# A fused chunk-attention and ELU-FFN kernel: the attention of early tiles in quarters with one transfer of v each, and the loads of later tiles' q and k taken apart

## Chip, cores and metric

One core of a Trainium2 chip runs the whole kernel. The metric is the device time of one execution in microseconds, as the median of several runs; lower is better.

## What is computed

Attention within chunks of 64 tokens, 8 heads of width 64, followed by a feed-forward layer with ELU, all in float32. q and k are drawn 5.7 times larger than in the function below.

```python
B, H, S, D = 8, 8, 576, 64            # q, k, v; chunk = 64, so 9 chunks per sequence
scores = scale * np.matmul(q_c, k_c.transpose(0, 1, 2, 4, 3))
scores = scores - np.max(scores, axis=-1, keepdims=True)
attn = np.exp(scores)
attn = attn / (np.sum(attn, axis=-1, keepdims=True) + 1e-09)
out = np.matmul(attn, v_c)            # then [B, S, H*D] flattened to x: 4608 tokens x 512
h = x @ w_in                          # 512 x 2048
g = np.where(h > 0.0, h, np.exp(np.minimum(h, 0.0)) - 1.0)
return g @ w_out                      # 2048 x 512
```

The weights come as float64 words; the kernel turns each into a float32 value and splits it into two parts (names ending in `_hi` and `_lo`) whose products TensorE takes at its fast rate; x and the hidden values are split in the same way, and `three` (L431) issues three matmuls for one product.

## The kernel before

The 4608 tokens are 36 tiles of 128, that is two chunks each, in nine blocks of four tiles. Attention of a block's tiles is worked out while the block before it is in the feed-forward part, except for the first four tiles, which have nothing to hide behind: this is the **start**. The order of the work on PE, ACT, DVE and SP is written out by hand in strings, one item for one step of a generator, so each engine takes its instructions in just that order.

The start follows `LOADS` (order of the transfers on SP) and `START`. In `START` a digit is the next step of that tile's attention, `r` one step of weight preparation on ACT (`prepare_units`, L140 and L145), `d` one step of weight splitting, mostly on DVE (`split_units`, L160 to L188), and `wN` N transposes of a constant on PE, whose result is not used (`warm`, L677). `uN` in `LOADS` is weight unit N: a slice of `w_in` and, from unit 1, one of `w_out`. Unit u+2 is loaded from step `d` of unit u.

The attention of a tile (`early_attention`) has ten steps: 1 transposes of q and k on PE (L266); 2 copies out of PSUM on ACT (L275, L278), where k is spread over a zeroed tile of twice its size (`kbd`, `k_apart`) so that one matmul of 128 rows serves two heads; 3 scores (L313); 4 maximum and subtraction on DVE (L319, L333); 5 exp on ACT (L337), or with `by_head` eight exps that take the maximum and give the sum of a head each (L327); 6 sums, reciprocal and product on DVE (L339 to L341, L282); 7 four transposes of the result on PE (L286); 8 a copy on ACT (L289); 9 the product with v (L297); 10 x is put away by ACT (L423, L417), in the start with a second half on DVE (L424). The product with v reads v in an arrangement that takes four transfers (`load_v`, L230).

The first block follows `FIRST_BLOCK`: H is the hidden product of one of 16 slices of w_in, P the projection of the slice before, and a a step of the next block's tile, whose loads are issued at the second a of the tile before. In blocks 1 and 2, and from block 3 on, tiles 8 to 35 go through `later_attention`, which transposes q and k on DVE (L358), computes scores and x in quarters of 64 rows by 64 columns of PE (L364, L406), and turns the softmax through eight small transfers within the chip (L397) and a DVE transpose (L399).

From block 3 on the feed-forward part uses a scheme with seven products per pair of slices. Its operands are read from DRAM again for each block, in four transfers a pair (`load_operands`, L566, item `w`), which PE needs two pairs later. The strings for this are `PAIRS` (two pairs to a tile), `FIRST_PAIR`, `OPENING_PAIR` and `LAST_PAIR`. Item `L` issues the transfers of q and k of the next tile but one (`load_tokens`, L247: four for q and four for k, or eight and eight where the tile crosses the end of a sequence, as tiles 4, 13, 22 and 31 do); `l` issues v (L219); `n` is a step of the next tile, `a` one of the present tile. Outputs are stored from SP too (L481). SP works strictly in order.

Of the kernel before, what the change touches and what calls it, by code (L numbers as in the profile page):

```python
# [10 lines left out]
F32 = mybir.dt.float32  # L11
# [9 lines left out]
def kernel(  # L21
# [19 lines left out]
    nc = tc.nc  # L41
# [33 lines left out]
    ps_h = ctx.enter_context(tc.tile_pool(name="ps_h", bufs=2, space=bass.MemoryType.PSUM))  # L75
# [4 lines left out]
    k_apart = const.tile([P, NK, 2, P], F32, name="k_apart")  # L80
# [70 lines left out]
    def split_units():  # L151
# [13 lines left out]
        for u in range(NU):  # L165
# [13 lines left out]
            if u:  # L179
                yield from subtract(u - 1)  # L180
# [8 lines left out]
            yield  # L189
        yield from subtract(NU - 1)  # L190
# [10 lines left out]

    def chunk_of(n: int):
        b, s = divmod(n, S)
        return b, slice(s, s + C)
# [19 lines left out]
    def load_v(n0: int, pool):  # L224

        v_sb = pool.tile([P, NK, 2, D], F32, name="v_sb")
        for j in range(2):
            for c in range(2):
                b, ss = chunk_of(n0 + c * C)
                nc.sync.dma_start(  # L230
                    out=v_sb[j * C:(j + 1) * C, :, c, :],
                    in_=v[b, j::2, ss, :].rearrange("h s d -> s h d"),
                )
        return v_sb

    def load_tokens(n0: int, qk):
# [4 lines left out]
        for i, src in enumerate((q, k)):  # L241
# [18 lines left out]


    def front_tensor(q_sb, k_sb, kbd, at, psum):
        def transpose(src):
            ps = psum([P, NK, P])
            for hp in range(NK):
                nc.tensor.transpose(  # L266
                    out=ps[:, hp, :], in_=src[:, 2 * hp:2 * hp + 2, :], identity=ident
                )
            return ps

        q_ps = transpose(q_sb)
        k_ps = transpose(k_sb)
        yield
        qT = at.tile([P, NK, P], F32, name="qT")
        nc.scalar.copy(out=qT, in_=q_ps)  # L275
        for j in range(2):
            js = slice(j * D, (j + 1) * D)
            nc.scalar.copy(out=kbd[js, :, j, :], in_=k_ps[js])  # L278
        yield qT

    def back_tensor(a, z, v_sb, at, psum):
        nc.vector.tensor_tensor(out=a, in0=a, in1=z.broadcast_to([P, H, C]), op=ALU.mult)  # L282
        yield
        a_ps = psum([P, NK, P])
        for hp in range(NK):
            nc.tensor.transpose(out=a_ps[:, hp, :], in_=a[:, 2 * hp:2 * hp + 2, :], identity=ident)  # L286
        yield
        aT = at.tile([P, NK, P], F32, name="qT")
        nc.scalar.copy(out=aT, in_=a_ps)  # L289
        yield  # L290
        x_ps = psum([P, NK, P])
        for hp in range(NK):
            for c in range(2):
                cs = slice(c * C, (c + 1) * C)
                for j in range(2):
                    js = slice(j * D, (j + 1) * D)
                    nc.tensor.matmul(  # L297
                        x_ps[js, hp, cs], lhsT=v_sb[js, hp, c, :], rhs=aT[js, hp, cs],
                        start=True, stop=True,
                    )  # L300
        return x_ps

    def early_attention(tt: int, front, v_sb, kbd, at, psum, put, by_head: bool = False):

        next(front)
        yield
        qT = next(front)
        yield
        s_ps = psum([P, H, C])
        for hp in range(NK):  # L310
            for c in range(2):
                cs = slice(c * C, (c + 1) * C)
                nc.tensor.matmul(  # L313
                    s_ps[cs, 2 * hp:2 * hp + 2, :], lhsT=qT[:, hp, cs], rhs=kbd[:, hp, :, cs],
                    start=True, stop=True,
                )
        yield
        mx = sm.tile([P, H, 1], F32, name="mx")
        nc.vector.tensor_reduce(out=mx, in_=s_ps, axis=AX.X, op=ALU.max)  # L319
        a = at.tile([P, H, C], F32, name="a")  # L320
        z = sm.tile([P, H, 1], F32, name="z")
        if by_head:

            nc.vector.tensor_scalar_mul(mx, mx, -SCALE)
            yield
            for h in range(H):
                nc.scalar.activation(  # L327
                    out=a[:, h, :], in_=s_ps[:, h, :], func=AF.Exp, scale=SCALE,
                    bias=mx[:, h, :], accum_out=z[:, h, :],
                )  # L330
            yield
        else:
            nc.vector.tensor_tensor(  # L333
                out=a, in0=s_ps, in1=mx.broadcast_to([P, H, C]), op=ALU.subtract
            )
            yield
            nc.scalar.activation(out=a, in_=a, func=AF.Exp, scale=SCALE)  # L337
            yield
            nc.vector.tensor_reduce(out=z, in_=a, axis=AX.X, op=ALU.add)  # L339
        nc.vector.tensor_scalar_add(z, z, 1e-9)  # L340
        nc.vector.reciprocal(z, z)  # L341
        x_ps = yield from back_tensor(a, z, v_sb, at, psum)
        yield
        put((slice(None), slice(None), slice(tt * P, (tt + 1) * P)), x_ps)
        yield
# [673 lines left out]
```

## Time and profile before

| | us |
|---|---|
| Median of 3 runs (863.40, 864.01, 864.86) | 864.01 |
| The profiled execution's own time | 868.06 |
| Its span from the first to the last instruction | 866.30 |
| PE busy in that span | 847.7 (98%) |
| DVE, ACT, POOL busy | 508.9, 484.5, 217.4 |
| TensorE clock granted over the span | 0.994 of full speed |

All rows come from one profiled execution, whose time is 4.05 us above the median of the others. In rows of the timeline the first number is the start in us from the beginning of the span, the second the time from the start of the first to the end of the last instruction merged in the row, then come engine, line, operation, operands, the count, and in brackets the idle time before it with what ended it. PE is TensorE's matmuls, SPq the issue of transfers. Several rows of one engine overlap a little, so the distance from one start to the next is what an instruction costs.

### The profile page before, as it was taken

To read this page: it belongs to the slowest core of one execution; us is meant where nothing else is said; L and a number is where in the kernel's file an instruction comes from. 1 tells how busy PE (TensorE), PEld (TensorE's weight loads), DVE (VectorE), ACT (ScalarE), POOL (GpSimd) and SP (SyncE) were. 2 spreads that over 40 slices of the span, in tenths; PEclk is the share of its full clock that TensorE was granted. 3 is DMA by queue.
4 is the path that set the end of the run, shared out by engine and by line. 5 is a ranking of instruction groups with operands and counts; after the bars stand their busy time and mean duration, and the time that the engine had idled before them with its cause. 6 is when DMAs were issued, how large, how long until landed. Compare 5 with 4: busy or idle time off the path is not lost.

```text
span 866.3 us, 17307 instructions
## 1 busy us (share of the span) xinstructions
PE 847.7 (98%) x6622; PEld 732.8 (85%) x6622; DVE 508.9 (59%) x840; ACT 484.5 (56%) x933; POOL 217.4 (25%) x184
## 2 busy tenths in 40 slices
PE   7799999999999999999989999999999999999998
PEld 6678888888888888888878888888888988889997
DVE  5789996556766566456534674457556754542222
ACT  6799985344534346546635564556544645465443
POOL 2000003126223023224312242225222522252221
PEclk9899999999999999999999999999999999999999
DMA  7786552546467758887688868887869798557521
GB/s 192 198 256 198 186 151 74 163 127 198 151 220 227 222 171 252 255 241 222 196 254 265 249 214 260 258 253 222 279 202 271 214 289 271 191 195 240 171 86 49
DMA packets 156707, 180.47 MB, mean 208 GB/s; under 512 B 67024, under 2 KB 123344, under 8 KB 156624
## 3 DMA queue, kind: packets, MB, share of 16 engines
q1 hardware_dynamic: 156624, 179.36, 67.6%
q8 instruction: 52, 0.85, 0.4%
q14 instruction: 31, 0.25, 0.1%
HBM read 147.85 MB, written 24.12 MB: 199 GB/s over the span
## 4 chain that ended last, share of the span: by engine, by line
PE 90%; DMA 4%; SPq 2%; ACT 2%; DVE 1%; issue 0%; ACTq 0%
PE o L431 44%; PE h L431 41%; DMA st<-in_moe_w_out_dram 2%; PE ps_a L364 2%; DMA wi_hi<-a_dram 2%; PE ps_a L406 1%; SPq L219 1%; SPq L230 1%; PE ps_a L297 0%; PE ps_a L313 0%; SPq L119 0%; PE ps_a L266 0%; ACT st L140 0%; DMA y<-y 0%; ACT st L145 0%
## 5 line engine op out<-in xcount | busy, mean ns | idle before, releaser
L655 POOL TENSOR_TENSOR wi_lo<-e,wi_hi 128x512 fp32r<-128x512 f32 x84 | 108.6, 1293 | 331.5 <-ACT wi_hi L651 331.5
L431 PE MATMUL h<-xhi,wi_hi 128*128 128x256 f32 (+1 forms) x704 | 189.7, 315 | 0.0
L639 DVE TENSOR_TENSOR kept<-h,kept 128x256 f32<-128x256 f32 x144 | 60.9, 423 | 178.2 <-PE h L431 112.3
L634 ACT COPY kept<-h 128x256 f32<-128x256 f32 x192 | 70.2, 366 | 169.2 <-PE h L431 169.1
L431 PE MATMUL o<-wo_lo,wi_hi 128*128 128x512 f32 x384 | 152.5, 397 | 0.0
L431 PE MATMUL o<-wo_hi,wi_hi 128*128 128x512 f32 x384 | 152.3, 397 | 0.0
L431 PE MATMUL o<-wo_hi,wi_lo 128*128 128x512 f32 x384 | 149.7, 390 | 0.0
L431 PE MATMUL h<-xlo,wi_hi 128*128 128x256 f32 (+1 forms) x448 | 147.2, 329 | 0.0
L431 PEld LDWEIGHTS h<-xhi,wi_hi 128*128 128x128 f32 x704 | 124.0, 189 | 14.5 <-issue 0.3
L431 PE MATMUL h<-xhi,wi_lo 128*128 128x256 f32 (+1 forms) x448 | 131.4, 330 | 0.5 <-DVE wi_lo L160 0.5
L431 PEld LDWEIGHTS h<-xlo,wi_hi 128*128 128x128 f32 x448 | 84.5, 189 | 12.2 <-DVE xlo L424 0.2
L431 PEld LDWEIGHTS h<-wi_lo,wi_hi 128*128 128x128 f32 x576 | 81.8, 189 | 11.2 <-DMA wi_hi<-a_dram 2.2
L431 PEld LDWEIGHTS h<-xhi,wi_lo 128*128 128x128 f32 x448 | 79.7, 188 | 11.5 <-DVE wi_lo L160 0.9
L646 DVE SCALAR_TENSOR_TENSOR e<-e,kept 128x512 f32<-128x512 f32 x96 | 66.9, 697 | 36.2 <-ACT e L644 21.2
L431 PE MATMUL h<-wi_lo,wi_hi 128*128 128x256 f32 x576 | 85.0, 283 | 2.2 <-DMA wi_hi<-a_dram 2.0
L431 PEld LDWEIGHTS o<-wo_hi,wi_lo 128*128 128x128 f32 x384 | 72.3, 188 | 16.4 <-POOL wi_lo L655 0.3
L643 ACT ACTIVATE e<-kept 128x512 f32<-128x512 f32 x96 | 60.6, 632 | 34.7 <-DVE kept L639 34.6
L651 ACT CAST wi_hi<-e 128x512 fp32r<-128x512 f32 x96 | 59.8, 623 | 32.0 <-DVE e L646 31.6
L431 PE MATMUL o<-wo_hi,ghi 128*128 128x512 f32 x192 | 76.3, 397 | 0.0
L431 PEld LDWEIGHTS o<-wo_lo,wi_hi 128*128 128x128 f32 x384 | 73.8, 192 | 2.3
L507 POOL TENSOR_TENSOR kept<-wi_hi,wi_lo 128x512 f32<-128x512 f32 x16 | 20.8, 1323 | 216.7 <-DVE qT L358 132.6
L431 PEld LDWEIGHTS o<-wo_hi,wi_hi 128*128 128x128 f32 x384 | 72.7, 189 | 2.6
(100 smaller groups left out, 1379.7 us busy)
## 6 DMA issues: line engine op xcount, KB each, us to landing
wi_hi<-a_dram SPq DMA_DIRECT2D x128, 448.0 KB, 5.7
wi_lo<-a_dram SPq DMA_DIRECT2D x64, 448.0 KB, 5.5
kept<-in_q_dram SPq DMA_DIRECT2D x100, 128.0 KB, 7.2
kept<-in_k_dram SPq DMA_DIRECT2D x100, 128.0 KB, 4.9
st<-in_moe_w_in_dram SPq DMA_DIRECT2D x16, 512.0 KB, 4.2
st<-in_moe_w_out_dram SPq DMA_DIRECT2D x16, 512.0 KB, 4.9
a_dram<-kept SPq DMA_DIRECT2D x16, 512.0 KB, 4.3
y<-y SPq DMA_DIRECT2D x224, 32.0 KB, 1.9
```

What stands on the lines that cost most here:

```text
L219: nc.sync.dma_start(out=dst[p0:p0 + n], in_=src[b, :, s0:s0 + n, :].rearrange("h s d -> s h d"))
L230: nc.sync.dma_start(out=v_sb[j * C:(j + 1) * C, :, c, :], in_=v[b, j::2, ss, :].rearrange("h s d -> s h d"),)
L364: nc.tensor.matmul(scores[halves[c], j, hp, :], lhsT=qT[halves[j], hp, halves[c]], rhs=kT[halves[j], hp, halves[c]], start=True, stop=True,)
L406: nc.tensor.matmul(x_ps[halves[j], c, hp, :], lhsT=v_sb[halves[c], 2 * hp + j, :], rhs=turned[halves[c], j * NK + hp, :], start=True, stop ...
L431: nc.tensor.matmul(ps, lhsT=a, rhs=b, start=start, stop=stop, skip_group_check=onto)
L507: nc.gpsimd.tensor_tensor(out=out, in0=a, in1=b, op=op)
L634: nc.scalar.copy(out=out, in_=self.x)
L639: nc.vector.tensor_tensor(out=out, in0=self.y, in1=self.kept[kept], op=ALU.add)
L643: nc.scalar.activation(out=e, in_=c, func=AF.Relu, scale=-1.0)
L646: nc.vector.scalar_tensor_tensor(out=e, in0=e, scalar=-1.0, in1=c, op0=ALU.add, op1=ALU.max)
L651: nc.scalar.copy(out=ghi, in_=e)
L655: engine.tensor_tensor(out=glo, in0=e, in1=ghi.bitcast(F32), op=ALU.subtract)
```

## The change

The early tiles (0 to 7) take on the quarter scheme of the later ones. q and k are transposed into the two banks of one PSUM tile; k is copied as it is, without the spreading and the zeroed tiles; scores and the product with v are 64x64 quarters; the softmax is turned by sixteen 64x64 matmuls with a constant, in place of four transposes; v comes in one transfer with the form of q's. Two tiles of the start (2 and 3) use the exps by head. `LOADS` and `START` are rewritten, the start's PSUM is four tiles of two banks, the hidden products' PSUM is allocated after the start and no longer ahead of it, and the subtraction for weight unit 0 comes right after its copy. From block 3 on, `L` loads k of the next tile only and moves to the second pair of a tile, and a new item `M` at the end of that pair loads q of the tile after it.

```diff
-    LOADS = "q0 k0 q1 k1 k2 q2 u0 q3 k3 v3 v0 u1 v2 v1"
+    LOADS = "q0 k0 q1 k1 q2 k2 u0 v0 q3 k3 v1 v2 v3 u1"
+    BY_HEAD = (2, 3)
     START = (
-        "w13 0 0 1 1 0 1 0 2 1 0 2 2 0 r 3 0 1 d 2 3 3 2 1 2 0 0 3 2 0 r 1 w7 3 d 2 r 1 "
-        "2 3 r w1 d 3 3 d d 1 d 1 3 2 w8 3 r r d w1 d d d"
+        "w13 0 0 1 1 0 0 2 1 1 0 2 r r d 0 2 2 1 d 3 0 0 3 1 3 3 2 0 0 d 1 1 2 3 1 1 2 2 d 3 "
+        "2 2 r r d w4 3 3 3 d 3 r r d d d d"
     )
...
+    def multiply_v(x_ps, v_sb, aT):
+        for hp in range(NK):
+            for c, j in quarters:
+                nc.tensor.matmul(
+                    x_ps[halves[j], c, hp, :], lhsT=v_sb[halves[c], 2 * hp + j, :],
+                    rhs=aT[halves[c], j * NK + hp, :], start=True, stop=True,
+                )
...
+    def early_attention(tt: int, q_sb, k_sb, v_sb, kT, at, pool, put, by_head: bool):
+        both = pool.tile([P, 2, DM], F32, name="ps_a")
...
+        for i, to in enumerate((qT, kT)):
+            nc.scalar.copy(out=to, in_=both[:, i, :].rearrange("p (h t) -> p h t", h=NK))
+        yield
+        scores = first_halves(both)
+        score(scores, qT, kT)
+        yield
...
+        turned_ps = both[:, 0, :].rearrange("p (h t) -> p h t", h=H)
+        for h in range(H):
+            for half in halves:
+                nc.tensor.matmul(
+                    turned_ps[half, h, :], lhsT=a[half, h, :], rhs=ident[half, half],
+                    start=True, stop=True,
+                )
+        yield
...
-        "p1 c1 x1 Q p2 d1 w B Q p6 c2 B Q B x2 p5 w x3 n n Q p7 c3 d2 A w a Q Q L p4 c4 A w Q p3 d3 "
+        "p1 c1 x1 Q p2 d1 w B Q p6 c2 B Q B x2 p5 w x3 n n Q p7 c3 d2 A w a Q Q p4 c4 A w Q p3 d3 "
         "A A Q B",
-        "n a a p1 c1 Q p2 d1 w B Q p6 c2 B Q B n n p5 w Q n p7 c3 d2 A w n l Q Q p4 c4 A w Q p3 d3 "
-        "A A Q B w",
+        "n a a L p1 c1 Q p2 d1 w B Q p6 c2 B Q B n n p5 w Q n p7 c3 d2 A w n l Q Q p4 c4 A w Q p3 d3 "
+        "A A Q B w M",
...
                     elif item == "L":
                         if n + 1 < NB * NTT:
-                            loaded = load_tokens((n + 1) * P, place_of_tokens(n + 1))
+                            loaded = load_tokens((n + 1) * P, place_of_tokens(n + 1), (1,))
+                    elif item == "M":
+                        m = n + 2 - (g == 0)
+                        if m < NB * NTT:
+                            load_tokens(m * P, place_of_tokens(m), (0,))
```

`OPENING_PAIR` loses its `L` as the first string of `PAIRS` does, `LAST_PAIR` is changed like the second, and `FIRST_PAIR` has `M` in the place of `L`. `load_v`, the spread tiles and their memsets on POOL go.

## Rows read from the trace of the kernel before

**Rows 1.** Timeline of PE, end of the start and first block.
```profile
24.60 2.20 PE L297 MATMUL ps_a<-qT,v_sb 64*64 64x64 f32 x32 [3.19 <-DMA v_sb<-in_v_dram]
...
32.29 0.47 PE L431 MATMUL h<-xhi,wi_hi 128*128 128x512 f32 x1
...
35.73 0.66 PE L266 MATMUL ps_a<-ident,q_sb 128*128 128x128 f32 x4 [0.38 <-DMA q_sb<-in_q_dram]
...
40.80 1.09 PE L313 MATMUL ps_a<-k_apart,qT 128*64 128x128 f32 x16 [0.72 <-issue]
```
**Rows 2.** Timeline of SP in the start.
```profile
6.26 0.90 SPq L119 DMA_DIRECT2D st<-in_moe_w_in_dram  x1
...
18.00 6.92 SPq L230 DMA_DIRECT2D v_sb<-in_v_dram  x8
```
**Rows 3.** Busy time by stretch: PE, PEld, DVE, ACT, POOL, PE clock, DMA share, GB/s.
```profile
32.30:60.00 27.70, 25.77 (x153) 20.18 (x154) 24.25 (x34) 25.66 (x51) 0.00 (x0) 1.00 0.76 223
...
430.00:460.00 30.00, 26.31 (x208) 23.02 (x207) 11.02 (x21) 11.96 (x25) 6.38 (x5) 0.94 0.79 243
```
**Rows 4.** What PE waited for from 138 us to the end: total, times, longest.
```profile
PE h L431 <- DMA wi_hi<-a_dram: 2.0, 1, 2.0
PE ps_a L406 <- DVE turned L399: 0.9, 1, 0.9
PE h L431 <- DMA wi_lo<-a_dram: 0.8, 1, 0.8
```
**Rows 5.** Timeline of SP ahead of these waits.
```profile
417.93 8.70 SPq L247 DMA_DIRECT2D kept<-in_q_dram  x8
...
430.48 0.37 SPq L566 DMA_DIRECT2D wi_lo<-a_dram  x1
...
434.67 7.20 SPq L397 DMA_DIRECT2D y<-y  x8
```
**Rows 6.** Timeline of DVE: the values that the transfers at 434.67 move.
```profile
427.45 0.75 DVE L388 TENSOR_TENSOR y<-ps_a,z 128x256 f32<-128x256 f32 x2
```
**Rows 7.** Transfer issued at 6.26: count, KB, us from issue to landing.
```profile
st<-in_moe_w_in_dram SPq DMA_DIRECT2D x1, 512.0 KB, 5.9
```
**Rows 8.** Timeline of DVE: step 6 of one tile, then the next.
```profile
15.80 0.68 DVE L339 TENSOR_REDUCE z<-a 128x8 f32<-128x512 f32 x1
...
17.56 0.68 DVE L339 TENSOR_REDUCE z<-a 128x8 f32<-128x512 f32 x1
```
**Rows 9.** Timeline of ACT: a copy, a wide preparation, exps by head, what follows.
```profile
17.39 0.58 ACT L289 COPY qT<-ps_a 128x512 f32<-128x512 f32 x1
...
24.39 1.13 ACT L140 ACTIVATE st<-st 128x1024 f32<-128x1024 f32 x1 [2.52 <-DMA st<-in_moe_w_out_dram]
...
43.32 0.31 ACT L327 ACTIVATE a<-ps_a,mx 128x64 f32<-128x64 f32 x1 [0.17 <-DVE mx L324]
...
45.73 0.65 ACT L456 CAST ghi<-e 128x512 fp32r<-128x512 f32 x1
```
**Rows 10.** Timeline of PE: steps 3, 7 and 9 of an early tile with the matmul after each.
```profile
92.99 1.09 PE L313 MATMUL ps_a<-k_apart,qT 128*64 128x128 f32 x16
94.01 0.50 PE L431 MATMUL o<-wo_hi,ghi 128*128 128x512 f32 x1
...
99.59 0.60 PE L286 MATMUL ps_a<-ident,a 128*128 128x128 f32 x4
99.94 0.48 PE L431 MATMUL o<-wo_hi,ghi 128*128 128x512 f32 x1
...
105.61 1.15 PE L297 MATMUL ps_a<-qT,v_sb 64*64 64x64 f32 x32
106.69 0.50 PE L431 MATMUL o<-wo_hi,ghi 128*128 128x512 f32 x1
```
**Rows 11.** The same for scores in quarters of a later tile.
```profile
140.90 0.69 PE L364 MATMUL ps_a<-k_apart,qT 64*64 64x64 f32 x32
141.53 0.50 PE L431 MATMUL h<-xhi,wi_hi 128*128 128x512 f32 x1
```

More of the change, by code (lines that the diff above doesn't have):

```diff
@@ L189, in split_units @@
             yield
+            if u == 0:
+                yield from subtract(0)
         yield from subtract(NU - 1)
@@ L222, in load_heads, with load_tokens @@
         return dst
[L224 to L236, printed above, removed]
+    def load_tokens(n0: int, qk, which=(0, 1)):
         U = 4
-        for i, src in enumerate((q, k)):
+        for i in which:
+            src = (q, k)[i]
             for j in range(2):
@@ L281, in back_tensor @@
[L281 to L345, printed above, removed]
@@ L347, in later_attention @@
-    def later_attention(tt: int, qk, v_sb):
-        halves = [slice(i * C, (i + 1) * C) for i in range(2)]
-        quarters = [(0, 0), (1, 1), (0, 1), (1, 0)]
-        qT = at.tile([P, NK, P], F32, name="qT")
-        kT = k_apart.rearrange("p h j t -> p (h j) t")[:, :NK, :]
-        for i, to in enumerate((qT, kT)):
-            nc.vector.transpose(out=to.rearrange("p h (t u) -> p h u t", u=4), in_=qk[:, i])
-            yield
-        banks[:] = [ps_a.tile([P, 2, DM], F32, name="ps_a")]
-        scores = banks[0][:, :, :NK * C].rearrange("p j (h t) -> p j h t", h=NK)
+    halves = [slice(i * C, (i + 1) * C) for i in range(2)]
@@ L362, in later_attention, with score @@
+    quarters = [(0, 0), (1, 1), (0, 1), (1, 0)]
+    def score(scores, qT, kT):
         for hp in range(NK):
@@ L368, in later_attention @@
+    def later_attention(tt: int, qk, v_sb):
+        qT = at.tile([P, NK, P], F32, name="qT")
+        kT = k_turned
+        for i, to in enumerate((qT, kT)):
+            nc.vector.transpose(out=to.rearrange("p h (t u) -> p h u t", u=4), in_=qk[:, i])
+            yield
+        banks[:] = [ps_a.tile([P, 2, DM], F32, name="ps_a")]
+        scores = first_halves(banks[0])
+        score(scores, qT, kT)
         yield
@@ L760 @@
         tc.tile_pool(name="start", bufs=NTT) as start,
-        tc.tile_pool(name="ps_start", bufs=6, space=bass.MemoryType.PSUM) as ps_start,
+        tc.tile_pool(name="ps_start", bufs=NTT, space=bass.MemoryType.PSUM) as ps_start,
     ):
         make_identity(nc, ident)
-        kbds = [start.tile([P, NK, 2, P], F32, name="kbd") for _ in range(NTT)]
-        for kbd in kbds:
-            nc.gpsimd.memset(kbd, 0.0)
         loaded = {}
@@ L771 @@
                 load_unit(n)
[L772 to L782 removed]
+            else:
+                loaded[item] = load_heads(
+                    {"q": q, "k": k, "v": v}[kind], f"{kind}_sb", n * P, start)
+        tiles = [early_attention(
+            tt, *[loaded[f"{kind}{tt}"] for kind in "qkv"],
+            start.tile([P, NK, P], F32, name="kT"), start, ps_start, split_first_x, tt in BY_HEAD,
+        ) for tt in range(NTT)]
         for item in START.split():
```

137 lines of the change are left out of this document (74 added, 63 removed).

## Prediction

> **What bounds the kernel now.** I read the profile from the whole to the part: busy time, then busy time by stretch, then PE's timeline where it is not full. PE is busy for 847.7 of 866.3 us, so the only time to be had lies in PE's gaps and in PE work that goes. [...] **First, the start.** Until the first hidden product, at 32.29 us, PE works on four tiles of attention and waits; the last long wait, 3.19 us, is for v [rows 1]. The reader sees why on SP: the last eight of sixteen transfers of v take 6.92 us to issue and run until 24.92 [rows 2]. **Second, the first block to 60 us.** PE is idle for 1.93 us, while ACT is busy for 25.66 and DVE for 24.25 of 27.70 us [rows 3], so two engines beside PE are nearly full; the gaps that show are at 35.73, for q of tile 4, and at 40.80, where the scores wait for ACT's copies [rows 1]. [...] The softmax that the eight small transfers carry is ready at 428.20 [rows 6]; SP turns to them at 434.67, 6.5 us late [rows 5].
>
> **PE work of the early tiles.** Counted from start to start with the matmul behind, the scores cost 1.02 us, the four transposes 0.35 and the product with v 1.08 [rows 10]. Scores in quarters cost 0.63 [rows 11], and I take the product with v in quarters for the same. The sixteen 64x64 matmuls for turning are new. Their nearest row is the old product with v: as many instructions of the same shape that also alternate between two diagonal quarters, 1.08; the lower bound is the quarters' 0.63, as if all four overlapped. Before: 1.02 + 0.35 + 1.08 = 2.45. After: 0.63 + 1.08 + 0.63 = 2.34, with 1.89 as the lower end. So one tile gains 0.11 us (0.56 at best), and the four tiles that lie in the full first block 0.4 us. The full-array transposes ran on with no gap ahead of them while every 64-row group shows about 0.1 us more at its edges, which takes that 0.4 back. I put this part at 0, from -1.8 to +0.4.
>
> [...]
>
> **The start, step by step.** Up to weight unit 0 nothing new is ahead on SP, so unit 0 lands as before, at 6.26 + 5.9 = 12.16 us [rows 2, 7]. Behind it 256 KB transfers follow at some 223 GB/s [rows 3], 1.2 us each: k of tile 3 at about 15, v of tile 3 at about 18.5. Before, v was the last thing; now v is there ten us early, and I ask what is late next. It is ACT, through the exps by head and the written order.
> DVE splits unit 0 (from 12.95) ahead of tile 0's step 6, which takes 17.56 - 15.80 = 1.76 us [rows 8] and ends at 15.1. PE turns tile 0 behind tile 3's transposes, from 15.5 to 16.6. ACT copies it (0.58, [rows 9]) and tile 3's q and k, to 18.2. The exps by head of tile 2 take 45.73 - 43.32 = 2.4 us [rows 9], to 20.6. Then x of tile 0 on ACT, its lower half and the last step of unit 0 on DVE, and the copy of unit 0 on ACT, 0.6 each: 23.1. Tile 1's copy and tile 3's exps: 23.6, 26.0. Tile 1's x and tile 2's copy: 27.0; tile 2's product with v on PE, 27.8, and its x: 28.3. Two wide preparations of unit 1 at 1.05 a step [rows 9]: 30.4. Tile 3's copy, its product with v, its x on ACT and the lower half on DVE: 0.6 each, with 0.2 for PE to drain, 33.0. The hidden product needs that lower half from its second matmul on, and its PSUM is tile 3's, so it cannot start ahead either. Against 32.29 this is 0.7 us later. PE is idle for about 3 us ahead of 23.6 in this chain, as it is now ahead of 24.60, behind which 32 matmuls took 2.20 us [rows 1] against 1.15 at full speed [rows 10]; with the same behind the new gap PE's groups on the chain grow by 0.5 to 1 us: 33.0 to 34. The memsets that go are POOL's, and nobody waits for POOL once the constant is made; the exps by head also take 1.3 us a tile off DVE, which has idle time there and is not what ends last. Both cost or give nothing.
>
> **The first block** gives this back. Unit 3 and tile 4's q, k and v are issued from 22.5 us on rather than behind sixteen v transfers, so the idle time at 35.73 and the one for k behind it go, 0.7 us of bare idle and about 1.05 with the slower restart. ACT has one copy less for each tile (0.6), but stands as far behind at the first hidden product as it does now: it must still prepare units 2 and 3, copy unit 1 and do the first ELU ahead of tile 4's copies. Adding these up gives the scores of tile 4 at 40.5 to 41.2, against 40.80 [rows 1]. That is the step at which a later start is absorbed, since ACT and DVE bound PE there [rows 3]. Start and first block together: +0.2 us, from -1.5 to +2. What hides the later start is that ACT queue; if the cover is gone, the 0.7 to 1.7 us count in full.
>
> **The loads taken apart.** As many transfers are issued, and SP passes all 16 for tile 22 between the same two groups of small transfers. What moves: the eight of q go ahead of the block's boundary, past the first four operand loads and the stores of the old block, and the eight of k behind these, ahead of three operand loads. Their waits then overlap: SP does q's while it would have waited for the stores of 417.5 and 431. From 415.1 (the last operand load ahead of M): q to 421 to 424, three operand loads, stores and the fourth load 2.6 us, k 3.7 to 5, three loads 2.1: the small transfers at 430 to 433.5 in place of 434.67. The fourth load goes from 430.48 to about 423, which ends the wait of 0.8; 2 us earlier are enough for the 0.9 and the 2.0, and without idle PE the clock does not fall. Value: -5.5; the other end is 0 (the small transfers 1 us earlier, waits that move only), or +2 (k's delay comes on top). I take -4.7, nearer the full removal. Queued behind L and M on SP are operand loads, small transfers and stores; PE waits for the first two.
>
> **Sum.** The profiled execution: 868.06 + 0 + 0.2 - 4.7 = 863.6. It stands 4.05 us above the median, and three runs of 863.4 to 864.9 cannot each hold much that it lacks: either profiling slows all of it, then the stall is in the timed runs too, and 864.01 - 4.5 = 859.5; or the timed runs have only 5.5 - 4.05 = 1.45 of it, and 864.01 + 0.2 - 1.45 = 862.8. Nothing here decides; I take the middle, **861.0**, with 858 to 863.
>
> **Rivals.** (1) *The stall is the profile's alone*, or its waits only move: 864.01 + 0.2, some 864.2, no change. For: the profiled run is the slow one. Against: the 16 transfers and their order are the program's. (2) *The start becomes ACT's, and slower*: its place is the exps by head of tiles 2 and 3, each 2.4 us on ACT where one exp takes about 0.6, so 3.6 us on the queue that ends last. It decides as soon as the first hidden product is more than about 1.5 us late, past what tile 4's scores absorb; at 35 us, with a stretch at the lower clock like that of rows 3 behind it (1.8), it costs 3, giving 867 without the stall's gain. For: the chain above is ACT's from 16.7 on. Against: preparation of later units is there to absorb it. (3) *The start is shorter*, because ACT is less bound than I wrote: first hidden product at 30, nothing absorbed: -2.3, and with the stall 857 to 859. Against: unit 0's landing does not move. (4) *K and q in new places hold up operand loads or small transfers*: 866. (5) *The warm-up is too short.* Seventeen unused transposes between 20 and 32 us become four. If the clock has not risen again by the first hidden product, that runs at the lower level for a stretch like the one of rows 3: +1.8, 865.8 without the stall's gain. For: fewer matmuls behind the gap. Against: the turning matmuls and the products with v fill much of that time.
>
> **How the numbers follow.** Forecast 0.50, rival 1 0.22, rival 2 0.10, rival 3 0.08, rival 4 0.06, rival 5 0.04. This kernel's measurement can tell 0.2%, 1.7 us, from no change. Faster is most of the forecast and rival 3: 0.45 + 0.08 = 0.53. Same is the rest of the forecast, nearly all of rival 1 and parts of 2 and 5: 0.31. Slower 0.16. The range reaches from the forecast with a somewhat shorter start, 857.5, to a slower start without a gain, 865.8.
>
> **What would show it.** Right: the first hidden product at 32.5 to 34 us with ACT full from 17 us on and no wait for v; tile 4's transposes with no wait and its scores near 41; turning at 1.0 to 1.1 us a tile; no wait for `a_dram` near 430 to 450, SP at the small transfers by 433. Wrong: a first hidden product before 31 or after 35, a stall that is only moved, or a median that falls as little as the start alone would give.

## The result, and the profile after

The change makes the kernel slower: a median of 866.76 us (864.3 to 870.01, 16 executions) against 863.62 us for the kernel before in 16 executions beside it, a ratio of 1.0039 with a 95% interval of 1.0031 to 1.0048. A second set on another chip gave 865.18 against 862.88 us, 1.0024 (1.0011 to 1.0036). The profiled execution of the changed kernel took 867.18 us with a span of 865.4.

The two profiled executions differ by 0.9 us only (868.06 to 867.18), and this small difference is the sum of two large ones of opposite sign, a start that is 3.4 us longer and a stall (the waits of [rows 4], between 430 and 460 us) that is 4.3 us shorter. First the timeline of PE after (start us, us, engine, line, operation, idle time ahead of it and what ended it), with the steps of [rows 1] and [rows 11]:

```profile
34.95 0.79 PE L404 MATMUL h<-xhi,wi_hi 128*128 128x512 f32 x1 [1.43 <-DVE xlo L396]
...
39.97 0.60 PE L275 MATMUL ps_a<-ident,q_sb 128*128 128x128 f32 x4
...
44.05 0.69 PE L253 MATMUL ps_a<-k_turned,qT 64*64 64x64 f32 x32 [0.26 <-ACT k_turned L282]
...
144.31 0.69 PE L253 MATMUL ps_a<-k_turned,qT 64*64 64x64 f32 x32
```

The first hidden product is at 34.95 (32.29 before), tile 4's scores at 44.05 (40.80), and the first later tile's scores at 144.31 (140.90). The waits for v and for tile 4's q are gone, as forecast; the start is later all the same. Between tile 4's scores and tile 8's lie 100.26 us after and 100.10 before: the first block neither loses nor gains, and the whole delay goes through.

Next the ELU of the first hidden product, the step on ACT that starts the way to tile 4's scores. The timeline of ACT in the kernel before:

```profile
35.32 1.17 ACT L140 ACTIVATE st<-st 128x1024 f32<-128x1024 f32 x1 [0.45 <-DMA st<-in_moe_w_out_dram]
36.37 0.59 ACT L448 ACTIVATE e<-h 128x512 f32<-128x512 f32 x1
```

and after:

```profile
40.23 0.60 ACT L421 ACTIVATE e<-h 128x512 f32<-128x512 f32 x1 [1.90 <-PE h L404]
```

Before, ACT comes to it with no idle time, so ACT's own queue sets it (the preparation ahead of it had waited 0.45 us for a load). After, ACT has stood idle for 1.90 us and waits for PE. The thing that should have hidden a late product was not there.

Last, busy time by stretch (columns as in [rows 3]), and PE's waits from 138 us to the end, as in [rows 4]:

```profile
32.30:60.00 27.70, 25.35 (x215) 20.22 (x216) 22.41 (x33) 23.45 (x48) 0.00 (x0) 0.87 0.55 167
...
430.00:460.00 30.00, 28.84 (x234) 25.43 (x234) 13.12 (x27) 14.78 (x30) 6.48 (x5) 1.00 0.91 270
```

```profile
PE ps_a L261 <- DVE turned L377: 0.7, 1, 0.7
PE h L404 <- DMA wi_hi<-a_dram: 0.5, 1, 0.5
```

In 32.3 to 60 us PE is idle for 2.35 us and its mean clock is 0.87, where it was 1.00. In 430 to 460 us the idle time is 1.16 us in place of 3.69 and the clock stays at 1.00. By the starts of the tiles' scores, before has two periods there that exceed the usual 22.38 us, by 1.07 and 4.89, and after has one, by 1.63: 4.3 us less.

### The profile page after: what moved, and what is told of

Same layout as the page of the kernel before. It is cut to its first block, busy times and chain, and to the rows that moved or that the text cites. A ratio compares the mean times of both kernels' runs of the same rounds, so it can differ in the third digit from the quotient of the medians.

```text
span 865.4 us, 17940 instructions
## 1 busy us (share of the span) xinstructions
PE 845.8 (98%) x6961; PEld 730.3 (84%) x6961; DVE 505.5 (58%) x838; ACT 482.8 (56%) x955; POOL 212.6 (25%) x179
## 4 chain that ended last, share of the span: by engine, by line
PE 92%; DVE 2%; ACT 2%; DMA 1%; SPq 1%; issue 1%; DVEq 0%; ACTq 0%
PE o L404 45%; PE h L404 42%; PE ps_a L253 2%; PE ps_a L261 2%; SPq L216 1%; PE ps_a L320 1%; ACT a L298 1%; DMA k_sb<-in_k_dram 1%; DMA wi_hi<-a_dram 1%; PE ps_a L275 0%; DVE xlo L396 0%; ACT e L422 0%; DVE y L180 0%; ACT qT L327 0%; ACT e L421 0%
## 5 line engine op out<-in xcount | busy, mean ns | idle before, releaser
L404 PE MATMUL o<-wo_lo,ghi 128*128 128x512 f32 x192 | 74.9, 390 | 0.0
```

Of the source, the lines that this page charges most:

```text
L404: nc.tensor.matmul(ps, lhsT=a, rhs=b, start=start, stop=stop, skip_group_check=onto)
```

## The experiments

All kernels compute the whole result. The table has, for each profiled execution, the starts (us) of the first hidden product (H0), of tile 4's transposes behind its twelve matmuls (T4), of the first ELU on ACT (E), of tile 4's scores (S4) and of tile 8's (S8), and the ratio of the timed runs to the kernel before on the same chip, with its 95% interval.

| kernel | H0 | T4 | E | S4 | S8 | ratio |
|---|---|---|---|---|---|---|
| before | 32.29 | 35.73 | 36.37 | 40.80 | 140.90 | 1 |
| after | 34.95 | 39.97 | 40.23 | 44.05 | 144.31 | 1.0039 (1.0031, 1.0048) |
| a0_after | 33.13 | 37.55 | 37.81 | 41.62 | 141.88 | 1.0024 (1.0011, 1.0036) |
| e1_whole_exps | 32.62 | 37.38 | 37.64 | 41.47 | 141.70 | 1.0012 (1.0001, 1.0024) |
| e2_warm | 34.89 | 37.74 | 38.09 | 41.89 | 142.18 | 1.0017 (1.0004, 1.003) |
| e3_loads_together | 33.29 | 37.73 | 37.99 | 41.81 | 142.07 | 1.0017 (1.0006, 1.0029) |
| e7_three | 34.52 | 37.34 | 37.70 | 41.52 | 141.81 | 1.0017 (1.0005, 1.003) |
| e4_loads_apart | 29.15 | 34.13 | 34.74 | 40.00 | 139.31 | 1.0008 (0.9999, 1.0018) |
| e5_first_block | 29.93 | 36.02 | 36.38 | 41.72 | 141.33 | 0.9992 (0.9981, 1.0003) |
| e6_old_order | 29.36 | 33.68 | 33.97 | 37.80 | 138.06 | 0.9940 (0.9920, 0.9959) |
| e6_again | 29.07 | 32.27 | 32.60 | 36.50 | 136.62 | 0.9966 (0.9952, 0.9979) |
| e8_order_only | 31.45 | 34.27 | 34.57 | 38.39 | 138.68 | 0.9994 (0.9981, 1.0007) |
| e9_puts_first | 27.52 | 30.93 | 31.93 | 35.75 | 135.98 | 0.9960 (0.9944, 0.9976) |
| e10_old_order_apart | 29.93 | 32.79 | 33.08 | 36.88 | 137.12 | 0.9962 (0.9949, 0.9975) |
| f0_own_order | 35.01 | 39.45 | 39.71 | 43.55 | 143.78 | 1.0024 (1.0011, 1.0037) |
| f1_unit_later | 32.23 | 36.59 | 38.22 | 42.03 | 142.31 | 1.0041 (1.0026, 1.0056) |
| f2_puts_gathered | 32.99 | 37.73 | 38.99 | 42.78 | 143.05 | 1.0025 (1.0010, 1.0039) |
| f3_unit_earlier | 32.93 | 35.78 | 36.21 | 40.05 | 140.29 | 1.0020 (1.0007, 1.0034) |
| f4_old_unit_later | 27.69 | 31.75 | 33.35 | 37.17 | 137.43 | 0.9964 (0.9952, 0.9976) |
| e10_again | 29.40 | 33.81 | 34.07 | 37.90 | 138.17 | 0.9955 (0.9941, 0.9970) |

Two columns are worth subtracting. In the sixteen profiles besides after that have the changed early tiles in start and first block, S4 - E is 3.79 to 3.90 us (3.82 after) and S8 - S4 is 100.1 to 100.3. So E fixes the start's cost, and E is the later of two things: PE's twelve matmuls, and ACT's queue. From S8 to the end of the span, all profiles take 719.2 to 721.7 us but two, before's (725.4, with the stall) and e7_three's (723.5, with several short waits). So what differs between the kernels lies in the main ahead of S8. Most medians are of 12 executions; those of e6_old_order, e10_old_order_apart, e9_puts_first, f1_unit_later and e10_again are of 5 to 8.

### The change again, and the exps whole

> The changed kernel itself, beside the experiments on the same chip. Theory start: ratio to the kernel before 1.003 to 1.004, with tile 4's scores 1.5 to 3 us later than in the kernel before; how late the first hidden product is differs from execution to execution with the place where the clock falls. Theory chip (the 0.4% was of the other chip): under 1.002, as for the version with the loads together (1.0017).

The second set of the same kernel. H0 is 1.8 us earlier than in the first profile, so the start of one kernel differs by that much between two profiled executions, which were on two chips. S4 is only 0.82 us later than in the profile of before, where I had put 1.5 to 3. The kernel stays slower.

```diff
-    BY_HEAD = (2, 3)
+    BY_HEAD = ()
```

> The changed kernel with the exps of the start's tiles 2 and 3 taken whole again, as one ACTIVATE of 128x512 (0.63 us) for eight by head (2.4 us); nothing else differs. Theory ACT (the start is late because 3.6 us of exps lie on the ACT queue that ends last): the first hidden product moves from 34.95 to about 32, and the time falls by 2 to 3 us from the changed kernel's 866.8, to some 864, ratio to the kernel before 1.000 to 1.002. Theory clock (the start is late and its first product slow because TensorE's clock falls in the gaps): the product moves by under 1 us, since DVE takes over 2.6 us of the same chain, the gaps stay, and the time is 866 to 867, ratio 1.003 to 1.004.

Beside the first profile these are the numbers of theory ACT: H0 falls from 34.95 to 32.62, and the ratio is 1.0012. But a0_after, which has the exps by head, has H0 at 33.13. Against it ACT has 3.5 us less to do from 16 us to S4 (17.2 in place of 20.7 busy), and S4 comes only 0.15 us earlier: in the changed order ACT waits for PE in the time that it saves (1.61 us ahead of E, 1.26 in a0_after). By the ratios 0.1% is gained against a0_after, where the intervals overlap, and 0.27% against the first set, where they do not. f0_own_order, below, has whole exps too and stands at 1.0024. So the exps by head are at most a part of what makes this start slow.

### More unused transposes

```diff
-        "w13 0 0 1 1 0 0 2 1 1 0 2 r r d 0 2 2 1 d 3 0 0 3 1 3 3 2 0 0 d 1 1 2 3 1 1 2 2 d 3 "
-        "2 2 r r d w4 3 3 3 d 3 r r d d d d"
+        "w13 0 0 1 1 0 0 2 1 1 0 2 r r d 0 2 2 1 d 3 0 0 3 1 3 3 2 0 0 d 1 1 w6 2 3 1 1 2 2 w8 d 3 "
+        "2 2 r r d w7 3 3 w4 3 w9 d 3 r r d d d d"
```

> The changed kernel with 34 unused transposes in place of 4 in the gaps of PE between the second turning and the first hidden product; nothing that other engines do differs. Theory clock: the granted clock is full when the first hidden product begins, its twelve matmuls take 2.7 us in place of 5.0 and tile 3's turning and product with v 1.3 us less; the time falls by 2.5 to 4 us to some 863 to 864, ratio 0.999 to 1.001. Theory ACT: the order of ACT's queue sets the first block's time whatever the clock, since unit preparation stands in the same queue; the time stays at 866 to 867, ratio 1.003 to 1.004.

PE's busy time, clock, DMA share and GB/s from 32.5 to 38 us, first of this kernel and then of e3_loads_together, whose start is the changed kernel's:

```profile
32.50:38.00 5.50, 4.93 (x56) 1.00 0.58 135
```

```profile
32.50:38.00 5.50, 4.71 (x15) 0.69 0.98 258
```

The granted clock is 1.00 over this stretch where e3's is 0.69, and the twelve matmuls take 2.85 us (34.89 to 37.74) in place of 4.44 (33.29 to 37.73). But the product starts 1.6 us later, and T4 is the same to 0.01 us. What the clock gives, the later start takes. How much of the later start is due to the transposes on PE, and how much to the difference between executions, these two profiles do not tell; e7_three, with transposes too, has H0 at 34.52. The ratio of 1.0017 lies between the two theories and overlaps with that of a0_after (1.0024), so no gain is shown.

### The loads

> The changed kernel with the loads of later tiles' q and k together again, at their old place. Theory start (all of the loss is in the start, and taking the loads apart does nothing in the timed runs, whose kernel before has no stall near 433 to 454 us): 866.8, ratio 1.003 to 1.005; a profile may show the stall or not. Theory loads (the loads in their new places hold up other transfers and cost a part of the loss): 864.5 or less, ratio under 1.002. Theory gain (the loads apart do gain, and the start lost more than is seen): 869 or more, ratio over 1.006.

> The kernel before with only the loads of later tiles' q and k taken apart, start and early tiles as they were. Theory start: no difference from the kernel before, ratio 0.999 to 1.001. Theory loads: 2 us or more above it, ratio over 1.002. Theory gain (the stall of the profile is in the timed runs too and goes): 3 to 5 us below it, ratio 0.994 to 0.997.

e3 is the changed kernel with `L` and `M` as before (one `L` for q and k); e4 is the kernel before with only `L` and `M` changed. Busy time from 430 to 460 us, first e3, then e4:

```profile
430.00:460.00 30.00, 30.00 (x245) 26.83 (x245) 14.74 (x26) 14.38 (x30) 7.36 (x6) 1.00 0.86 270
```

```profile
430.00:460.00 30.00, 28.04 (x232) 24.91 (x232) 13.63 (x24) 12.35 (x26) 6.63 (x6) 1.00 0.79 240
```

With the loads together PE is never idle there, with the loads apart it is idle for 1.96 us, against 3.69 in the profile of before, which also has them together. e7, with the loads together, has waits of 0.55 and 0.65 us there, 1.20 in all, and after, with the loads apart, 1.16 us of idle PE. The other profiles of both kinds take 719.2 to 721.7 us from S8 to the end, against 725.4 with the stall. The long stall belongs to one execution, not to an order of loads. e3's ratio of 1.0017 is the number of theory loads; but against a0_after (1.0024) the difference lies within the intervals, and e4, with the loads apart alone, loses nothing that can be measured: 1.0008 (0.9999 to 1.0018).

### The first block alone, and three parts undone

> The kernel before with only the tiles 4 to 7 in quarters and with one transfer of v each; the start, its order and the later loads as they were. Theory start (the whole loss is the start's): no loss here, ratio 0.998 to 1.000, by 0.05 us less PE work a tile, one copy less on ACT and three transfers less on SP per tile. Rival (the turning in 64x64 matmuls costs more on PE than the quarters give back): ratio 1.001 or more, periods of the first block longer than 25.7 us.

This is the kernel before with quarters and one transfer of v for tiles 4 to 7 only. Its ratio of 0.9992 (0.9981 to 1.0003) says that the early tiles' new form costs PE nothing and gives nothing, though here its scores also waited for loads of tile 4 that came late (T4 waited 2.94 us for q).

> The changed kernel with three undone at once: exps whole, unused transposes in PE's gaps, later loads together; the order of the start stays. If the three gains seen one by one (0.27%, 0.22% and 0.22% against the changed kernel) add up: ratio 0.996 to 0.998. If they share a cause, each only taking a part of the same delay in the start: ratio 1.000 to 1.002.

Whole exps, more unused transposes and loads together, in the changed order: still 1.0017. Of the changed start there were left the written order, the quarters with one transfer of v, `LOADS` and the PSUM tiles; the next runs keep all of these but the order.

### The order of before with the new attention

```diff
     START = (
-        "w13 0 0 1 1 0 0 2 1 1 0 2 r r d 0 2 2 1 d 3 0 0 3 1 3 3 2 0 0 d 1 1 2 3 1 1 2 2 d 3 "
-        "2 2 r r d w4 3 3 3 d 3 r r d d d d"
+        "w13 0 0 1 1 0 1 0 2 1 0 2 2 0 r 3 0 1 d 2 3 3 2 1 2 0 0 3 2 0 r 1 3 d 2 r 1 "
+        "2 3 r d 3 3 d d 1 d 1 3 2 w8 3 r r d w1 d d d"
     )
```

e6 has this order, whole exps and loads together; e10 the same with the loads apart; e8 is the changed kernel with this order alone.

> The changed kernel with the order of steps in the start that the kernel before has (less its unused transposes in the middle), the exps whole, and the later loads together; quarters, single transfers of v and the order of the transfers stay. Theory order (the written order in which ACT and DVE meet, with weight units 0 and 1 ahead of tiles 1 to 3, makes the start late, not v and not the quarters): tile 4's scores by 39 us, ratio 0.995 to 0.999. Theory quarters (the steps themselves are longer: turning on PE, more in one PSUM tile): no better than the version with whole exps, ratio 1.000 to 1.002.

> The kernel with the old order, whole exponentials and loads together once more, beside the three others of this set on one chip. Theory: 0.994 of before again, within 0.992 to 0.996, tile 4's scores at 37.5 to 39 us. Rival (its gain was that chip's or those executions'): 0.997 to 1.001.

> The changed kernel in everything (quarters, one transfer of v, two tiles' exponentials by head, q and k taken apart) but for the written order of the start, which is the order of before without its two unused transposes in the middle; the unused transposes share one finished tile. Theory (the new order lost the start: unit 0's five engine steps between the tiles' softmax, unit 1's two preparations ahead of tile 3's copies): the first hidden product is back at 29 to 31 us, tile 4's scores at 38 to 39, and the time at 0.994 to 0.996 of before, since the whole exponentials of the run with the old order were worth 0.3 us at the start and the loads nothing. Rival (it was the combination with whole exponentials and loads together that gained): scores of tile 4 at 40 to 42 and a ratio of 0.998 to 1.001.

> The kernel with the old order and whole exponentials, now with the changed kernel's loads of q and k taken apart; beside the run with the loads together on the same chip. Theory (the loads taken apart decide nothing in the median): both within 0.1% of each other, about 0.994 of before. Rival 1 (the loads apart gain where the stall at 420 to 450 us is in the timed runs): 4 us, 0.5%, faster, 0.989. Rival 2 (their transfers are late because they lie on SP behind the operands' places): slower than the loads together by 0.1% to 0.3%, 0.995 to 0.997.

e6 is 0.6% faster than before, and 0.34% in the second set, a little outside what I had put; e10 gives the same (0.9962), so the loads do nothing here either. e8 shows that order and exps go together: 0.9994, that is 0.30% less than a0_after by the order alone, and 2.7 us (0.32%) more than e10, whose only difference is whole exps. The ratio of e8 is thus the rival's, though S4 (38.39) is the theory's. In the old order the exps by head cost: PE waits 2.04 us in e8 for a tile's copy on ACT, and 0.20 in e10, and H0 comes 1.52 us later; E stands 0.3 us behind T4 in both. My expectation that the exps would cost some 0.3 us was wrong.

```diff
-        "2 3 r d 3 3 d d 1 d 1 3 2 w8 3 r r d w1 d d d"
+        "2 3 r d 3 3 d d 1 1 3 2 w8 3 w8 d r r d d d d"
```

> The kernel with the old order, with one step of DVE for unit 1 (1.23 us) moved behind the differences that the first hidden product waits for, and eight more unused transposes ahead of that product. In the run with the old order PE waited 2.10 us for the difference xlo, and the clock fell to the lower level at 30.4. Theory (the chain from ACT and DVE to S4 sets the start, and S4 waits on ACT's copy of k): the first hidden product comes 1 to 1.2 us earlier, at 28.2 to 28.5, tile 4's scores 0 to 0.6 us earlier, since ACT's copy at 37.2 stands behind unit 1's roundings which wait on the moved step; the time 0.9935 to 0.995 of before. Rival (PE's own order sets the scores): they come 1.1 to 1.5 us earlier and the time falls by 0.15%, to 0.992 to 0.993.

One step of unit 1 on DVE goes behind the lower halves, and there are more unused transposes: H0 comes 1.55 us earlier than in e6_again and S4 0.75, but the time is the same (858.95 and 858.80 us).

### Which step of the order

> The changed kernel's own order with whole exponentials, with unit 1's two preparations on ACT moved from ahead of tile 3's copy to behind its last step. In an earlier run of that order they held ACT from 29.57 to 31.7, but PE had turned tile 3 only at 31.0. Theory (the order loses by making each tile's last step wait for the one before): only some 0.6 us come back; the first hidden product at 31.5 to 32.3 (32.62 with these preparations ahead), tile 4's scores at 40.5 to 41.3, the time at 1.0003 to 1.0012 of before. Rival (these two preparations are what the order lost): the product 2.1 us earlier, at 30.5, scores at 39.4, and 0.998 to 0.999.

> The same, and the last steps (x to its two halves on ACT and DVE) of tiles 1, 2 and 3 gathered behind tile 3's product, as the order of before has them, so that tile 3's step 6 on DVE no longer stands behind tile 1's lower half, which waits for PE and ACT. Theory: the three chains overlap again, the first hidden product at 30 to 31, tile 4's scores at 38.5 to 39.7, the time at 0.997 to 0.999. Rival (the loss is earlier, in unit 0's steps and the interleaving of tiles 0 to 2 up to 20 us): within 0.5 us of the run with only the preparations moved, and 1.000 to 1.001.

f1 moves unit 1's preparations behind tile 3's last step, f2 also gathers the tiles' last steps. Both theories behind them fell: 1.0041 and 1.0025, and neither rival's ratio came. In f1 H0 came at 32.23 as expected, and S4 0.56 us later than in e1, because ACT had to catch up. The timeline of ACT in f1:

```profile
31.35 1.13 ACT L139 ACTIVATE st<-st 128x1024 f32<-128x1024 f32 x1
...
38.22 0.60 ACT L421 ACTIVATE e<-h 128x512 f32<-128x512 f32 x1
...
41.39 0.59 ACT L282 COPY k_turned<-ps_a 128x512 f32<-128x512 f32 x1
```

E waits for nothing here: T4 is at 36.59, and ACT gets to E 1.6 us later. So the first hidden product alone is not the mark.

Four more runs cross the two orders with an early and a late place of unit 1's two preparations, all with whole exps, on one chip:

> The changed kernel's order with whole exponentials and with unit 1's two preparations where the change has them (late, ahead of tile 3's copy): first corner of two orders by two places of these preparations. Expected as the earlier run of that kernel: first hidden product at 32 to 33.5, tile 4's first transposes at 37 to 37.8, its scores at 41.3 to 42, time 1.001 to 1.002 of before. Both theories expect this.

> The same order with unit 1's two preparations moved earlier, into the two gaps of 1.1 and 1.25 us that ACT had ahead of tile 2's copy and of its x. Theory (tile 4's scores come some 4.1 us behind its transposes, and these behind the first hidden product, unless ACT is full in between; the preparations only set the second): the product stays at 32 to 33, the scores at 41.2 to 41.8, the time within 0.1% of the run before. Rival (what the new order lost is the place of the preparations): scores at 39.0 to 39.8, and 0.25% faster than the run before.

> The order of before with unit 1's preparations moved behind the tiles' last steps, as the first of these runs nearly has them. Theory: the first hidden product comes as early as in the order of before or earlier, 27.5 to 30, but ACT is then full up to tile 4's copies, and the scores come 10.7 us behind the first preparation as in two earlier runs, at 37.2 to 39.1, 0.5 to 2 us later than with the early preparations; the time 0.05% to 0.25% longer than that kernel. Rival (the order of the tiles is all): scores at 35 to 37, the time the same or less.

> The order of before with whole exponentials and early preparations once more, on the same chip: the fourth corner. First hidden product at 29 to 30.5, tile 4's scores at 36.5 to 38, time 0.995 to 0.9975 of before.

| median us (mean granted clock of the runs) | preparations late | preparations early |
|---|---|---|
| order of the change | 865.30 (0.992) | 864.23 (0.992) |
| order of before | 860.00 (0.997) | 859.13 (0.998) |

The written order is worth 5.1 to 5.3 us, the place of the preparations about 1 us, within the intervals. The two orders differ in the order of the tiles' steps, in the place of unit 0's steps and in the unused transposes (17 and 22); these were not tried one by one. (In f3's own profile S4 came 1.2 us ahead of what I had expected, as its twelve matmuls ran in 2.85 us. f0's profile came some 2 us later than expected: its H0 of 35.01 stands beside 32.62 in e1, the same kernel, on another chip, but for the tile that the unused transposes write.) The kernel before had a mean clock of 0.997 beside these runs, so the clock goes with the order too.

The rows show where the orders differ on PE. PE of the changed kernel (L320 turns a tile, L261 is its product with v):

```profile
24.45 0.69 PE L261 MATMUL ps_a<-qT,v_sb 64*64 64x64 f32 x32 [1.68 <-ACT qT L327]
24.97 1.10 PE L320 MATMUL ps_a<-ident,a 64*64 64x64 f32 x32
27.79 0.69 PE L261 MATMUL ps_a<-qT,v_sb 64*64 64x64 f32 x32 [1.72 <-ACT qT L327]
...
29.67 1.97 PE L320 MATMUL ps_a<-ident,a 64*64 64x64 f32 x32 [0.60 <-DVE a L313]
32.38 1.13 PE L261 MATMUL ps_a<-qT,v_sb 64*64 64x64 f32 x32 [0.74 <-ACT qT L327]
```

and of e10_again:

```profile
19.38 2.41 PE L320 MATMUL ps_a<-ident,a 64*64 64x64 f32 x64
21.85 0.69 PE L261 MATMUL ps_a<-qT,v_sb 64*64 64x64 f32 x32
23.66 1.29 PE L320 MATMUL ps_a<-ident,a 64*64 64x64 f32 x31 [1.12 <-DVE a L313]
24.74 0.27 PE L261 MATMUL ps_a<-qT,v_sb 64*64 64x64 f32 x3
24.79 0.22 PE L320 MATMUL ps_a<-ident,a 64*64 64x64 f32 x1
24.85 0.63 PE L261 MATMUL ps_a<-qT,v_sb 64*64 64x64 f32 x29
25.74 0.70 PE L261 MATMUL ps_a<-qT,v_sb 64*64 64x64 f32 x32 [0.26 <-ACT qT L327]
```

In the changed order PE turns a tile, waits for ACT's copy, does its product with v, and only then turns the next tile, so the tiles pass one behind the other: their products are 3.3 and 4.6 us apart (24.45, 27.79, 32.38). In the order of before two tiles are turned together (x64) and the next one before the second product, so one tile's copy lies beside another's turning. The rows show no turning that starts ahead of a product which still waits (1.68 and 1.72 us). Out of the written order stands, in these rows, one matmul of 32: in e10_again the last of the turning from 23.66 on starts at 24.79, behind the first three of the product at 24.74.

PE's order is not the whole of it. ACT of the changed kernel (L187 is a copy of weight unit 0, L327 the copy of a turned tile):

```profile
23.30 0.62 ACT L187 CAST wi_hi<-y 128x512 fp32r<-128x512 f32 x1 [1.36 <-DVE y L180]
23.82 0.58 ACT L327 COPY qT<-ps_a 128x512 f32<-128x512 f32 x1
```

and of e10_again:

```profile
21.23 0.57 ACT L327 COPY qT<-ps_a 128x512 f32<-128x512 f32 x1
...
22.73 0.58 ACT L327 COPY qT<-ps_a 128x512 f32<-128x512 f32 x1
...
24.25 0.61 ACT L187 CAST wi_hi<-y 128x512 fp32r<-128x512 f32 x1
```

The copy for which the product at 24.45 waits stands on ACT behind unit 0's copy, which itself waits 1.36 us for DVE. Other profiles of the changed order have the same: ACT waits 1.35 to 1.67 us at this place in after, e1, e7, f1, f2 and f3, and the product of tile 1 waits 0.86 to 2.55 us for its copy in after, e7, f0, f1, f2 and f3. In the order of before unit 0's copy comes behind the copies of tiles 2 and 1. The next turning, at 24.97, could have come 0.67 us earlier at most, since DVE gave its values at 24.30. So there are two readings of what the order does wrong, the order of turnings and products on PE and the place of unit 0's steps between the tiles' steps (the rival named with f2). Both are read from the rows, neither was tried alone, and f1 and f2 leave both as they were. That the written order is the cause is shown; which of its steps stays open.

## Why the prediction was wrong

**What was right.** The wait for v went and tile 4's transposes waited for nothing. The PE work of the early tiles was put at 0 and is: from S4 to S8 PE is busy for 99.44 us after, 99.59 before (in e4 the whole stretch takes 99.31), and the ratio is 0.9992 alone. Turning costs what its nearest row said, 1.08 [rows 10], here from 102.31 to 103.38 in a tile of the first block:

```profile
101.76 0.39 PE L404 MATMUL h<-xlo,wi_hi 128*128 128x512 f32 x1
101.99 0.39 PE L404 MATMUL h<-xhi,wi_lo 128*128 128x512 f32 x1
102.31 1.15 PE L320 MATMUL ps_a<-ident,a 64*64 64x64 f32 x32
103.38 0.50 PE L404 MATMUL o<-wo_hi,ghi 128*128 128x512 f32 x1
103.72 0.39 PE L404 MATMUL o<-wo_lo,ghi 128*128 128x512 f32 x1
```

The chain of the start came in the forecast order, some 0.7 us later than put up to unit 1's preparations (ending at 31.1 in place of 30.4) and 1 to 2 us at its end. The memsets cost nothing.

The edges of the turning group show in the rows from 101.76 to 103.72. It starts 0.32 us behind the matmul ahead of it, and the matmul behind it is followed after 0.34 us, where two matmuls of the full array start 0.23 us apart (the first two). So one more group a tile outside the full array has some 0.1 us at each edge, and the first block's 99.44 us of busy PE show that it decided nothing.

**The step that failed: "The first block gives this back".** The forecast had the first hidden product 0.7 to 1.7 us late and all but 0.2 us of it absorbed in ACT's queue. Measured against before: H0 +2.66; the twelve matmuls behind it 5.02 us (34.95 to 39.97, granted clock 0.53) against 3.06 (32.29 to 35.35, where PE began to wait for q, clock 1.00), +1.96; absorbed -0.76, since before's E at 36.37 stood only that far behind the moment when PE was ready (35.35, and 0.26 as in after); one copy of k less, -0.61. That makes +3.25 for tile 4's scores, which the rows give too (44.05 - 40.80). So the product's delay was mis-sized by a microsecond, the matmuls behind it were left at their old time though [rows 1] already showed 2.20 us (at a granted clock of 0.50) for a group worth 1.15 behind a gap, and the cover was 0.76 us where the argument needed 1.5 or more. In a0_after the same sum is +0.84 + 1.36 - 0.76 - 0.61 = +0.83: there the product's delay lies within the forecast, and the slow matmuls alone take back what was to absorb it. This term, which the forecast had at nothing, is the one that failed in both profiles. I had written that ACT "stands as far behind" as it does now; the row of E would have told how far.

**The second failure: the middle between two readings of the stall.** The loads were put at -4.7, out of 5.5 us that the sum gives to the stall. These are [rows 3] added up: 30.00 - 26.31 = 3.69 us of idle PE, and 30 x (1 - 0.94) = 1.8 us for the clock (also the 1.8 of rivals 2 and 5), which reads 0.50 from 451 to 453 us; no run shows the 5.5 us as a difference of times. Between the two profiles the stretch did fall by 4.3 us. With the start's 3.41 this gives -0.9, which is the difference of the two spans. But the sum was then carried to the median halfway between "in all runs" and "hardly in any" (the middle of 859.5 and 862.8 is 861.15; the forecast has 861.0). It is hardly in any: before's profiled execution stands 4.4 us above its median and after's 0.4 above its own, the stretch has no stall in e3, and the loads alone gain nothing. The small transfers for tile 22 were issued at 437.40; less the start's delay that is 434.0, against 434.67 [rows 5] and a forecast of 430 to 433.5. SP's timeline after:

```profile
417.64 6.39 SPq L233 DMA_DIRECT2D kept<-in_q_dram  x8
...
428.68 6.72 SPq L233 DMA_DIRECT2D kept<-in_k_dram  x8
...
437.40 6.76 SPq L375 DMA_DIRECT2D y<-y  x8
```

k's eight issues took 6.72 us where I had 3.7 to 5. So even this step moved the small transfers by 0.7 us only; what ended the waits in this one execution stays open. Without the 4.3 us, before's median plus the start is 863.62 + 3.41 = 867.0, and 866.76 was measured. That they agree so closely is partly luck: the same sum for the second set is 862.88 + 0.98 (S8 of a0_after less that of before) = 863.9, and 865.18 was measured.

**The rivals.** Rival 1 on the stall was right. Rival 2, a start that becomes slower, gave 867 and its conditions were met almost to the number (H0 at 35, the twelve matmuls behind it at a clock of 0.53, no gain from the stall). But its cause was wrong, so the number was luck: it put the price on the exps by head, and without them the changed order is still slow (e1 1.0012, f0_own_order 1.0024). The written order, which my chain had walked through step by step, was never set against the old one. What rival 5 named shows in the rows (with more unused transposes, e2_warm, the twelve matmuls take 2.85 us at a clock of 1.00 from 32.5 to 38 us, in e3 4.44 us at 0.69), but curing it brought no gain, as the product came 1.6 us later.

**The parts apart.** With whole exps and the order of before, the rest of the change (quarters, one transfer of v, the new `LOADS` and PSUM tiles) brings 0.34 to 0.60% (e6, e10 and their repeats); this rest was not taken apart, and the quarters of tiles 4 to 7 alone bring nothing (e5). The written order takes about 0.6% (5.1 to 5.3 us) with whole exps and 0.30% (against a0_after) to 0.45% (against the first set) with exps by head; the exps by head take 0.32% in the old order and 0 to 0.27% in the new one, by the sets that are compared. The loads are worth nothing that can be measured. So the new attention, less order and exps by head, brings what the forecast had for the whole change (0.35%, which it had put on the loads), and the order in which it was written down took that and more.

## What to carry to other kernels

When a change brings a new written order along with a cheaper form of the work, run the cheaper form in the old order first; here that version beats both. In a start where engines hand tiles to each other, look at what the written order of each engine has behind a wait: a product that waits for a copy (here 1.68 and 1.72 us), with the next tile's turning behind it, or a copy behind a weight step that waits for a third engine (1.36 us). In the changed order, which has both, the tiles' products lie 3.3 and 4.6 us apart. And before a late step is called absorbed, find the row at which the two paths meet and read off by how much the other one is later; that number is all that can be absorbed.

## What the hardware showed unexpectedly

The twelve matmuls of the first product took from 2.82 us (e7_three, e8_order_only) to 5.02 us (after), and 5.02 and 4.42 in two profiles of one kernel (after and a0_after). They are longer where the granted clock is lower: 0.53 over the 5.02 us of after, 1.00 where they take 2.85 us in e2_warm. The granted clock of a start is thus part of its time, and in these runs it mostly goes with the gaps that the order leaves on PE. The runs of the changed order have a mean clock of 0.991 to 0.993, and PE is idle between 16 us and S4 for 7.27 to 8.93 us in five of their profiles (after, a0, e1, f1, f2). In e2_warm and e7_three, whose gaps are filled, it is 0.996 with 5.47 and 4.81 us; in the old order with whole exps 0.997 to 0.998 with 3.14 to 4.81 (e6, e6_again, e9, e10); in e8_order_only, with the exps by head, 0.9945 with 6.05; in the kernel before 0.997 with 5.68. From 60 to 138 us, where PE is busy for all 78.00 us in before and in after, the clock is 1.00 in both. The same program's stall at 430 us was 5.5 us in one execution and is absent from the timed ones by their sum, so one profiled execution can carry several microseconds that no median has.
